# Sixteen basis sums of a weight pair moved to another phase, a room of its own for one pair, and two products swapped

## Chip, core and metric

One core of a Trainium2 chip runs the kernel. Time is device microseconds (us) from launch to end; lower is better. PE is TensorE, DVE is VectorE, ACT is ScalarE, POOL is GpSimd, and SP is the engine whose queue issues most DMAs.

## What is computed

A linear attention without softmax, normalized per head, then a SwiGLU feed-forward layer, all in 32-bit floats:

```
kv  = einsum('bhsd,bhse->bhde', k, v)           # 8 batches, 8 heads, 576 positions, 64 wide
out = einsum('bhsd,bhde->bhse', q, kv)
rms = sqrt(mean(out * out, axis=-1) + 1e-6)
x   = (out / rms * g_norm), heads side by side   # 4608 x 512
g, val = x @ w_gate, x @ w_val                   # 512 x 1536 each
result = (silu(g) * val) @ w_out                 # 1536 x 512
```

## The kernel before

The 4608 tokens go through in nine blocks of 512. Each block has an *up phase* (x times the gate and value weights, then silu and the product, which gives `h`, kept transposed as 12 slots of 128 rows) and a *down phase* (`h` times the output weights). Block 0 computes its up phase plainly. Blocks 1 and 2 use Strassen's method in Winograd's form: seven products in place of eight. Blocks 3 to 8 run in pairs and apply the method twice, one inside the other (class `Inner`, L807).

**Products and their order.** `Quad.multiply` (L661) issues one of the seven products P1 to P7. They are summed in PSUM in three banks: chain b takes P1, then P6, P7 and P4 on top; chain a takes P2; chain c takes P5, then P3 on top. Between two members of a chain the bank is read: after P7, ACT copies bank b (L711) and DVE adds bank c to the copy (`after7`), so P4 may write b only after the copy and P3 may write c only after the addition. `after4` (L724) takes silu on ACT and multiplies on POOL into the second half of the tokens of `h`; `after3` adds on DVE and multiplies on POOL into the first half. `h_sums` then forms two sums over `h` on DVE, which P5 and P6 of the down phase read.

In an up phase of blocks 1 and 2 there are six *weight pairs* (`j` = 0 to 5, called pair 1 to 6 in the change's name), each a unit `Up`. The order in `Up.sequence` is P1, P5, then P4 and P3 of the unit before, P6, P2, P7. After the last unit only its P4 and P3 are left. The down phase (`Ffn.down`) has a single unit: P1, P6, P5, P7, P2, P4, P3, 24 matmul records each; in between it calls steps of the next block's attention (`fill`): after P1 `whole` (heads, L431; squares, roots, scaling; transposes on DVE, L510), after P5 `place_x` (16 DMAs that put x in place, L522), after P2 `end` (gain on ACT, L529, and the sums over x on DVE).

**Basis sums.** The paired blocks need each weight pair as 7 x 7 pieces, sums of its quarters, in device memory (tensor `w`), from where a stream loads them. Blocks 1 and 2 make and send them on the side. For the products whose weights are themselves sums this is `leaf_steps`; for the others it is `kept_steps(j)`: two halves, each of four sums on DVE (three of 256 columns, one of 512) and two DMAs on SP, `(6,)` and `(7, 4, 5)` (L916). Its sums are written to a room, `xi_alone`, from which the DMAs read, so that the next pair's sum must wait until the DMA that reads the same piece has landed. Such steps stand in two lists, `making` and `later`; after each product `make` takes some of them (4 in block 1, 2 in block 2, 12 in a down phase), from `later` only when `making` is empty. Pairs 1 to 4 come in `later` of block 1, pairs 5 and 6 in `making` of block 2:

```
if p == 3:
    if self.j < NP - 2:
        ffn.later.extend(kept_steps(self.j))
...
for j in (NP - 2, NP - 1):
    ffn.making.extend(kept_steps(j))
```

**Rooms.** `ring()` gives one of five buffers of 128 x 2048 that rotate; the product units, the attention's q, squares and scaled heads, and `leaf_steps` all take them. `h_alone` holds `h` of blocks 0, 1 and 2; its last four slots belong to pairs 5 and 6 and are written late in an up phase.

**What sets the order.** Each engine's instructions are put in order by a scheduler from their place in the program and an estimate of when they can run; it may move an instruction ahead of others. `tc.issue_after(ins)` puts what is traced inside behind `ins` on `ins`'s engine. In block 2 DVE keeps program order through the up phase and PE through the whole block (`in_order`). A DMA waits on its queue for the landing of the eighth DMA before it, since there are eight landing semaphores in turn.

In block 2 the attention of block 3 is woven into the up phase by `ahead`: the visit of k and v (L370), 32 loads of q (L333, `load`), `turn_q` (transposes of q on DVE, L386), and `half`, the heads (L431) with what follows.

Of the kernel before, what the change touches and what calls it, by code (L numbers as in the profile page):

```python
# [14 lines left out]
P = 128  # L15
# [3 lines left out]
def kernel(  # L19
# [41 lines left out]
    nc = tc.nc  # L61
# [10 lines left out]
    NF = FF // P  # L72
    NP = NF // 2
# [35 lines left out]
    def span(at, size):  # L109

        return arena[:, int(at * KIB) : int((at + size) * KIB)]
# [8 lines left out]
    x_alone, xi_alone, h_alone = x_of(span(48, X)), xi_of(span(62, XI_)), h_of(span(73, H_))  # L120
# [31 lines left out]
    def ring():  # L152

        return r_pool.tile([P, 4, BLK], F32, name="r")
# [485 lines left out]
    class Quad:  # L640
# [11 lines left out]
        def multiply(self, p):  # L652
            name, first = CHAIN[p]
            if first:
                tiles = [PSUMS[name].tile([P, 2, HB], F32, name=name) for _ in range(1 + (name in self.apart))]
                self.ps[name], self.apart[name] = tiles[0], tiles[-1]
            banks = self.ps[name], self.apart[name]
            for e, i in self.order(p):
                lhsT, rhs = self.operands(p, e, i)

                self.ffn.multiplied = nc.tensor.matmul(  # L661
                    banks[e][:, e], lhsT=lhsT, rhs=rhs, start=first and i == 0 and (e == 0 or banks[0] is not banks[1]),
                    stop=i == self.steps - 1, skip_group_check=True,
                )
            getattr(self, f"after{p}", lambda: None)()
# [17 lines left out]
    class Up(Quad):  # L683
# [43 lines left out]
        def after3(self):  # L727
            add(nc.vector, self.u2, self.ps["c"], self.u2)
            mul(nc.gpsimd, self.h[:, :, 0:HB], self.s, self.u2)
            if self.j < NP - 1:  # L730
                self.ffn.owed = lambda: self.ffn.h_sums(self.j, 1, nc.vector)
            else:
                self.ffn.ended = self.ffn.h_sums(self.j, 1, nc.vector)

        def multiply(self, p):
            super().multiply(p)
            ffn = self.ffn
            if ffn.n == 1:
                if p == 5:
                    self.leaf_room = ring().rearrange("p f (s c) -> p (f s) c", c=P)  # L740
                if p in (5, 7, 4):
                    at = 3 * (5, 7, 4).index(p)
                    ffn.making.extend(leaf_steps(self.j, [(self.w[p].unsqueeze(1), (p,))], self.leaf_room[:, at:]))
                if p == 3:
                    if self.j < NP - 2:
                        ffn.later.extend(kept_steps(self.j))

    class Inner:

# [164 lines left out]
    def send_leaf(j, os, ps, src):  # L914
        dst = stream.dram[:, j, steps_of(OUTERS, os), steps_of(INNERS, ps)].rearrange("p o i c -> p o (i c)")
        tc.keep_in_program_order(nc.sync.dma_start(out=dst, in_=src))  # L916
# [20 lines left out]
    def kept(j):  # L937

        halves = lambda t: t[j].rearrange("p (o i) (e c) -> p o i e c", o=2, e=2)
        return [(halves(wg), (1, 2)), (halves(wv), (6, 3))]  # L940

    def raw_steps(j):


        for t, os in kept(j):
            yield lambda t=t, os=os: send_leaf(j, os, (1,), t[:, :, 0, 0])
            yield lambda t=t, os=os: send_leaf(j, os, (2, 3), t[:, :, 1].rearrange("p o e c -> p o (e c)"))

    def kept_steps(j):


        room = xi_alone.rearrange("p a b c -> p (a b) c")
        for i, (t, os) in enumerate(kept(j)):
            b11, b12, b22 = t[:, :, 0, 0], t[:, :, 0, 1], t[:, :, 1, 1]
            to = room[:, 8 * i : 8 * (i + 1)].rearrange("p (o r) c -> p o r c", r=4)
            t2_ = to[:, :, 0]
            yield lambda b22=b22, b12=b12, t2_=t2_: sub(nc.vector, t2_, b22, b12)
            yield lambda b11=b11, t2_=t2_: add(nc.vector, t2_, t2_, b11)
            yield lambda t=t, t2_=t2_, to=to: sub(
                nc.vector, to[:, :, 2:4], t[:, :, 1], t2_.unsqueeze(2).to_broadcast([P, 2, 2, P])  # L960
            )
            yield lambda t2_=t2_, os=os: send_leaf(j, os, (6,), t2_)
            yield lambda b11=b11, t2_=t2_, to=to: sub(nc.vector, to[:, :, 1], b11, t2_)
            yield lambda to=to, os=os: send_leaf(
                j, os, (7, 4, 5), to[:, :, 1:4].rearrange("p o r c -> p o (r c)")
            )
        if j < 2:
            yield from raw_steps(j)
# [90 lines left out]
    class Ffn:  # L1059
# [27 lines left out]
        def up(self, fill):  # L1087

            self.s1 = s_pool.tile([P, NP, HB], F32, name="s1")
            units = [Up(self, j) for j in range(NP)]  # L1090
            units[0].prepare()
            last = None
            for i, this in enumerate(units):
                if i + 1 < len(units):
                    units[i + 1].prepare()
                for unit, p in this.sequence(last):
                    if unit:
                        visited, self.visited = self.visited, None
                        with tc.issue_after(visited.ins) if visited else ExitStack():
                            unit.multiply(p)  # L1100
                        self.make(4 if self.n == 1 else 2)
                        for steps, most in ((self.chores, 2), (self.sends, 10)):
                            for _ in range(min(most, len(steps))):
                                steps.pop(0)()
                    fill.get((i, p) if unit is this else None, lambda: None)()
                last = this
            self.down_ = Down(self)
            self.down_.turn_t(5)
            for unit, p in last.sequence(None):
                if unit is None:  # L1110
                    last.multiply(p)

        def down(self, nxt, then={}):

            down = self.down_
            fill = nxt.steps() if nxt else {}
            for p in (1, 6, 5, 7, 2, 4, 3) if 5 in fill else (1, 5, 6, 7, 2, 4, 3):
                if p == 1 and 7 not in down.t:
                    down.turn_t(7, self.ended)
                if p == 6 and 4 not in down.t:  # L1120
                    down.turn_t(4, nxt.halves[0] if nxt and nxt.n >= TURNED else None)

                with tc.issue_after(nxt.multiplied.ins) if self.n == 0 and p in (5, 6) else ExitStack():
                    down.multiply(p)
                self.make(12)
                if p in fill:
                    fill[p]()
                if p in then:
                    then[p]()
                if p == 1:  # L1130

                    with tc.issue_after(nxt.q_turned.ins) if self.n == 0 else ExitStack():
                        down.turn_s3()
# [109 lines left out]
    def ahead(ffn, att, then):  # L1243

        def load(att, i):
            return lambda: ffn.sends.extend(att.quarter_steps(i, (0, 1), (nc.sync,)))

        def first():
            visit(ffn, att, (0, 1))
            ffn.sends += [load(att, 0), lambda: then.load_kv(0), load(att, 1)]  # L1250

        def turn(i):
            ffn.chores.append(lambda: att.turn_q(i))

        def second():
            visit(ffn, then, (0,), True)
            ffn.sends.append(lambda: then.load_kv(1))

        def half(i):
            with tc.issue_after(ffn.multiplied.ins):  # L1260
                att.heads(i, range(NS), (m_psum, m_psum))
            ffn.visited = att.multiplied
            ffn.chores += att.chores(i)
            if i:
                ffn.chores += att.turn_steps()

        def rest():
            for i in range(2):
                load(then, i)()

        def raw():
            for j in range(2, NP):
                ffn.sends += raw_steps(j)

        def sums():
            ffn.chores.extend(att.sum_steps())

        for j in (NP - 2, NP - 1):
            ffn.making.extend(kept_steps(j))

        return {
            (0, 1): first, (1, 6): lambda: turn(0), (1, 7): second, (2, 1): lambda: half(0), (2, 6): lambda: turn(1),
            (2, 7): rest, (3, 1): lambda: half(1), (3, 7): lambda: visit(ffn, then, (1,), True), (4, 1): att.place_x,
            (4, 2): raw, (4, 7): att.gain_x, (5, 5): sums,
        }
# [133 lines left out]
```

## Time and profile before

| | before |
|---|---|
| median of 7 runs | 1024.88 us |
| lowest, highest | 1021.78, 1026.1 us |
| the profiled execution, its span | 1025.69 us, 1023.9 us |
| PE busy | 999.3 us, 98% of the span |
| DVE busy | 660.5 us, 65% |
| POOL busy | 367.8 us, 36% |
| ACT busy | 232.6 us, 23% |
| DMA | 143.23 MB, 140 GB/s on average |

Line numbers (L661 and so on) are those printed above. An instruction's row names its start and duration in us, its engine (a `q` behind it is the engine's queue, which waits or issues a DMA; PEld is a weight load of PE), its line, the operation, what it writes and reads (`out<-in`, by the program's names without buffer numbers), its shape and how many were merged; in brackets stands the idle time of the engine before it and what ended that. A float product is two matmul records, 0.2158 us apart at full clock; 24 records of the down phase take 5.18 us, the 8 of an up product 1.73 us.

Where the two blocks lie: block 1's up phase from 156.2, its down phase from 228.1 (the first matmuls of P1 stand before P4 there) to 273.9; block 2's up phase to 361.3, its down phase to 399.8.

### The profile page before, as it was taken

How to read it: one execution, taken by the hardware profiler on the slowest of the kernel's cores; microseconds unless marked ns; L12 is line 12 of the kernel's file. 1: busy time of each engine (PE TensorE's matmuls, PEld its weight loads, DVE VectorE, ACT ScalarE, POOL GpSimd, SP SyncE). 2: the span in 40 equal slices, each digit the busy share in tenths (PEclk: the TensorE clock that was granted, in tenths of full speed). 3: DMA queues.
4: the chain of work that ended last, by engine and by line, in shares of the span. 5: the costliest groups of instructions: out<-in, count | busy, mean ns of one | idle time of the engine just before them, and what ended most of it. 6: DMA issues, size and time to landing. Idle time of an engine off the chain costs nothing.

```text
span 1023.9 us, 17080 instructions
## 1 busy us (share of the span) xinstructions
PE 999.3 (98%) x6506; PEld 833.4 (81%) x6506; DVE 660.5 (65%) x1118; ACT 232.6 (23%) x367; POOL 367.8 (36%) x290
## 2 busy tenths in 40 slices
PE   5999999998989999999999999999999999999998
PEld 4544688887878888888888888888888888888887
DVE  2999797779347475666666846666767566666211
ACT  2666112221122312121111212112112121121100
POOL 0000273534534240454556003554650026546600
PEclk9999999999999999999999999999999999999999
DMA  8689643666564845676753365667321654443011
GB/s 219 199 265 265 124 90 115 217 206 174 116 146 77 212 86 162 172 204 163 169 145 50 89 159 152 160 172 183 98 34 51 144 159 146 150 148 94 1 42 42
DMA packets 254290, 143.23 MB, mean 140 GB/s; under 512 B 149504, under 2 KB 236544, under 8 KB 254208
## 3 DMA queue, kind: packets, MB, share of 16 engines
q1 hardware_dynamic: 219264, 137.67, 49.8%
q10 hardware_dynamic: 34880, 4.46, 2.7%
q8 instruction: 52, 0.85, 0.3%
q14 instruction: 30, 0.25, 0.1%
q0 software_dynamic: 64, 0.00, 0.0%
HBM read 104.99 MB, written 28.70 MB: 131 GB/s over the span
## 4 chain that ended last, share of the span: by engine, by line
PE 79%; DVE 10%; DMA 3%; SPq 3%; ACT 1%; issue 1%; POOL 1%; DVEq 0%; POOLq 0%; ACTq 0%
PE b L661 22%; PE b L807 22%; PE c L661 12%; PE c L807 11%; PE a L661 6%; PE a L807 5%; SPq L333 2%; DVE r L190 2%; DVE arena L131 2%; PE m L431 1%; PE m L370 1%; DVE arena L199 1%; DVE r L184 1%; DMA arena<-in_v_dram 1%; DMA ld<-in_v_dram 1%
## 5 line engine op out<-in xcount | busy, mean ns | idle before, releaser
L807 PE MATMUL b<-arena,t 128*128 128x256 f32 x1008 | 244.5, 381 | 0.0
L807 PEld LDWEIGHTS b<-arena,t 128*128 128x128 f32 x1008 | 190.0, 190 | 29.6 <-DVE r L130 2.4
L130 POOL TENSOR_TENSOR r<-r 128x256 f32<-128x256 f32 (+1 forms) x90 | 94.9, 1056 | 246.6 <-DMA t<-w 149.5
L130 DVE TENSOR_TENSOR r<-c,r 128x512 f32<-128x512 f32 (+1 forms) x170 | 104.8, 625 | 114.1 <-PE c L807 41.1
L130 DVE TENSOR_TENSOR r<-b,r 128x512 f32<-128x512 f32 (+1 forms) x234 | 139.1, 607 | 59.9 <-PE b L807 54.7
L131 POOL TENSOR_TENSOR t<-wo 128x512 f32<-128x512 f32 x54 | 76.1, 1429 | 181.0 <-DVE wo L130 104.6
L132 POOL TENSOR_TENSOR arena<-r 128x1024 f32<-128x1024 f32 (+1 forms) x54 | 101.7, 1897 | 104.3 <-DVE r L130 72.3
L130 DVE TENSOR_TENSOR r<-a,r 128x512 f32<-128x512 f32 x93 | 59.2, 637 | 114.3 <-PE a L661 77.6
L131 DVE TENSOR_TENSOR arena<-arena 128x512 f32<-128x512 f32 (+3 forms) x102 | 106.8, 1057 | 27.8 <-PE b L661 13.7
L807 PE MATMUL c<-arena,t 128*128 128x256 f32 x504 | 122.5, 379 | 0.8 <-ACT r L821 0.8
L807 PEld LDWEIGHTS c<-arena,t 128*128 128x128 f32 x504 | 95.6, 190 | 14.5 <-ACT r L821 1.2
L661 PE MATMUL b<-wo,arena 128*128 128x256 f32 x432 | 98.6, 382 | 2.6 <-issue 1.6
L661 PE MATMUL b<-t,arena 128*128 128x256 f32 x432 | 96.4, 379 | 1.4 <-POOL s L130 0.7
L661 PEld LDWEIGHTS b<-wo,arena 128*128 128x128 f32 x432 | 81.1, 190 | 15.3 <-issue 2.0
L661 PEld LDWEIGHTS b<-t,arena 128*128 128x128 f32 x432 | 81.9, 190 | 13.2 <-POOL s L130 1.1
L821 ACT COPY r<-b 128x512 f32<-128x512 f32 x54 | 31.7, 586 | 191.0 <-PE b L807 191.0
L131 POOL TENSOR_TENSOR t<-arena 128x512 f32<-128x512 f32 x36 | 50.4, 1412 | 63.5 <-PE c L661 26.0
L807 PE MATMUL a<-arena,t 128*128 128x256 f32 x252 | 66.1, 379 | 0.0
L807 PEld LDWEIGHTS a<-arena,t 128*128 128x128 f32 x252 | 47.9, 190 | 6.5
L661 PE MATMUL c<-wo,arena 128*128 128x256 f32 x216 | 48.2, 379 | 0.2 <-DVE r L130 0.2
L661 PE MATMUL c<-t,s 128*128 128x256 f32 x216 | 48.1, 379 | 0.0
L661 PE MATMUL a<-wo,arena 128*128 128x256 f32 x216 | 48.1, 379 | 0.0
(102 smaller groups left out, 1221.9 us busy)
## 6 DMA issues: line engine op xcount, KB each, us to landing
t<-w SPq DMA_DIRECT2D x180, 256.0 KB, 3.1
out_dram<-r SPq DMA_DIRECT2D x17, 512.0 KB, 2.9
ld<-in_k_dram SPq DMA_DIRECT2D x26, 288.0 KB, 4.8
ld<-in_v_dram SPq DMA_DIRECT2D x26, 288.0 KB, 5.9
t<-w SPq DMA_DIRECT2D x54, 128.0 KB, 2.2
ld<-in_moe_w_gate_dram SPq DMA_DIRECT2D x12, 512.0 KB, 4.9
ld<-in_moe_w_val_dram SPq DMA_DIRECT2D x12, 512.0 KB, 4.7
ld<-in_moe_w_out_dram SPq DMA_DIRECT2D x12, 512.0 KB, 5.0
```

The costliest lines, as they stand in the source:

```text
L130: add = lambda e, o, a, b: e.tensor_tensor(out=o, in0=a, in1=b, op=OP.add)
L131: sub = lambda e, o, a, b: e.tensor_tensor(out=o, in0=a, in1=b, op=OP.subtract)
L132: mul = lambda e, o, a, b: e.tensor_tensor(out=o, in0=a, in1=b, op=OP.mult)
L184: nc.vector.tensor_scalar(out=mag.bitcast(F32), in0=mag.bitcast(F32), scalar1=self.LOW, scalar2=self.HIGH, op0=OP.max, op1=OP.min,)
L190: return nc.vector.scalar_tensor_tensor(out=mag, in0=mag, scalar=3, in1=sign, op0=OP.logical_shift_left, op1=OP.bitwise_xor)
L199: return nc.vector.tensor_tensor(out=dst.bitcast(U32), in0=self.mag.rearrange("p (a b) -> p a b", a=a, b=b), in1=unit.bitcast(U32).rearran ...
L333: queue.dma_start(out=to[32 * r : 32 * (r + 1), j, g0:g1], in_=q[b, 4 * i + 2 * j + h, s0 : s0 + 32 * (g1 - g0), 32 * d : 32 * (d + 1)].re ...
L370: self.positions = nc.tensor.matmul(self.kv_ps[r][u * D : (u + 1) * D, g, :], lhsT=k[:, u, c, :], rhs=v[:, u, c, :], start=(c == 0), stop= ...
L431: self.multiplied = nc.tensor.matmul(self.ps[i][u][p : p + D, t, j, :], lhsT=self.qt[rows, tile_t, head, p : p + D], rhs=kvs[b % 3][rows, ...
L661: self.ffn.multiplied = nc.tensor.matmul(banks[e][:, e], lhsT=lhsT, rhs=rhs, start=first and i == 0 and (e == 0 or banks[0] is not banks[1 ...
L807: self.ffn.multiplied = nc.tensor.matmul(ps[:, i], lhsT=stream.use(self.ffn.n, self.j, o, p), rhs=self.operand(o, p), start=first and i == ...
L821: nc.scalar.copy(out=dst, in_=ps)
```

## The change

Three edits.

1. *Pairs 3 and 4.* `kept_steps` of `j` = 2 and 3 no longer enter `later` in block 1's up phase. They are traced in block 1's down phase, behind P5 (pair 3, room `xi_alone`) and behind P7 (pair 4, room `ring()`), each behind the scaling of block 2's heads on DVE (`nxt.scaled`) and the last x transfer on SP (`nxt.placed`).
2. *Pair 6.* `kept_steps` takes its room as an argument; for `j` = 5 that is the last four slots of `h_alone`. Pair 5 keeps `xi_alone`.
3. *Last unit.* In blocks 1 and 2 the last unit issues P3, then P4, then `h_sums` (`Up.end`), where before it issued P4, then P3 with `h_sums` in `after3`.

```
@@ class Up
             if self.j < NP - 1:
                 self.ffn.owed = lambda: self.ffn.h_sums(self.j, 1, nc.vector)
-            else:
-                self.ffn.ended = self.ffn.h_sums(self.j, 1, nc.vector)
+
+        def end(self):
+
+            for p in (3, 4):
+                self.multiply(p)
+            self.ffn.ended = self.ffn.h_sums(self.j, 1, nc.vector)
...
                 if p == 3:
-                    if self.j < NP - 2:
-                        ffn.later.extend(kept_steps(self.j))
+                    if self.j < 2:
+                        ffn.later.extend(kept_steps(self.j, chunks(xi_alone)))
@@
-    def kept_steps(j):
-
-
-        room = xi_alone.rearrange("p a b c -> p (a b) c")
+    def chunks(t):
+
+        return t.rearrange("p f (s c) -> p (f s) c", c=P) if len(t.shape) == 3 else t.rearrange("p a b c -> p (a b) c")
+
+    def kept_steps(j, room):
+
+
@@ class Ffn, up
             self.down_.turn_t(5)
-            for unit, p in last.sequence(None):
-                if unit is None:
-                    last.multiply(p)
+            last.end()
@@ class Ffn, down
+                if p in (5, 7) and self.n == 1:
+
+                    with tc.issue_after(nxt.scaled.ins), tc.issue_after(nxt.placed.ins):
+                        for step in kept_steps(2 + (p == 7), chunks(ring() if p == 7 else xi_alone)):
+                            step()
@@ ahead
         for j in (NP - 2, NP - 1):
-            ffn.making.extend(kept_steps(j))
+            ffn.making.extend(kept_steps(j, chunks(h_alone[:, NF - 4 :]) if j == NP - 1 else chunks(xi_alone)))
```

## The prediction

> **What bounds the kernel.** TensorE (PE) is busy 999.3 of 1023.9 us, so only its idle stretches, and any stretch at a lower clock, can be won. I first listed who PE waited for between 100 and 400 us (blocks 1 and 2 run from 156 to 400); columns: total, times, longest, in us.
>
> ```profile
> PE m L431 <- DVE r L386: 3.3, 1, 3.3
> PE b L661 <- issue: 1.6, 1, 1.6
> PE b L661 <- POOL arena L132: 1.0, 1, 1.0
> PE b L661 <- ACT r L711: 0.8, 1, 0.8
> PE c L661 <- DVE r L130: 0.5, 2, 0.3
> ```
>
> Five lines, 7.2 us, and one of them is half. Then the timeline around it (start, duration, idle time before and what ended it):
>
> ```profile
> 298.17 1.99 PE L661 MATMUL b<-arena 128*128 128x256 f32 x8
> 301.47 0.69 DVE L131 TENSOR_TENSOR arena<-arena 128x512 f32<-128x512 f32 x1 [5.36 <-DMA w<-arena]
> 302.08 1.24 DVE L386 STREAM_TRANSPOSE r<-ld 128x1024 f32<-128x1024 f32 x1
> 303.46 1.98 PE L431 MATMUL m<-kv,r 64*64 64x64 f32 x64 [3.29 <-DVE r L386]
> 305.38 3.78 PE L661 MATMUL c<-arena,t 128*128 128x256 f32 x8
> ```
>
> The heads of block 3 (L431) wait for a transpose of q (L386). VectorE (DVE), whose order is fixed in block 2, stood 5.36 us in front of it, at a basis sum of pair 6 that wants to overwrite a piece of the shared room which a DMA of pair 5 has not yet sent. Next the sums by stretch (length, then busy us of PE, its weight loads, DVE, ACT, POOL; then granted clock, DMA share, GB/s):
>
> ```profile
> 300.20:303.40 3.20, 0.00 (x0) 0.00 (x0) 1.93 (x3) 0.59 (x1) 0.00 (x0) 0.89 0.95 287
> 303.40:309.50 6.10, 6.04 (x74) 5.14 (x75) 3.73 (x11) 1.09 (x2) 0.20 (x1) 0.50 0.73 204
> 309.50:315.00 5.50, 5.50 (x27) 4.85 (x26) 2.05 (x4) 0.99 (x2) 4.79 (x4) 1.00 0.85 128
> ```
>
> The wait is paid twice: after it the clock is 0.50 until 309.5, though PE is busy. The queue of SP shows why the DMA was late:
>
> ```profile
> 281.05 10.99 SPq L333 DMA_DIRECT2D ld<-in_q_dram  x20
> 292.15 0.40 SPq L916 DMA_DIRECT2D w<-arena  x1
> 298.81 0.41 SPq L916 DMA_DIRECT2D w<-arena  x1
> ```
>
> The sends stand between 32 loads of q. Last, where the moved sums go, the down phase of block 1, first DVE, then GpSimd (POOL):
>
> ```profile
> 251.69 2.36 DVE L510 STREAM_TRANSPOSE r<-r 128x1024 f32<-128x1024 f32 x2
> 253.97 2.34 DVE L131 TENSOR_TENSOR arena<-arena 128x512 f32<-128x512 f32 x2
> 263.54 0.69 DVE L130 TENSOR_TENSOR r<-a,r 128x512 f32<-128x512 f32 x1 [7.22 <-PE a L661]
> 264.14 1.75 DVE L131 TENSOR_TENSOR arena<-arena 128x1536 f32<-128x1536 f32 x1
> 265.81 0.69 DVE L130 TENSOR_TENSOR r<-c,r 128x512 f32<-128x512 f32 x1
> ```
> ```profile
> 251.85 4.18 POOL L131 TENSOR_TENSOR t<-wo 128x512 f32<-128x512 f32 x3 [9.12 <-DVE r L132]
> 256.00 7.58 POOL L131 TENSOR_TENSOR t<-arena 128x512 f32<-128x512 f32 x6
> 265.37 5.00 POOL L131 TENSOR_TENSOR t<-arena 128x512 f32<-128x512 f32 x3 [1.80 <-PE b L661]
> ```
>
> DVE has a hole of 7.22 us there, but POOL works through nearly all of it.
>
> **Part 1: a room of its own for pair 6.** The four sums of each half of pair 6 now write the end of h, free since block 1's P3 (ended 273.9). No sum before the transpose overwrites pair 5's unsent pieces, so the 5.36 us go. What is late next? The transpose needs the first 16 of the 32 q loads; SP had issued 20 by 292.04 and such a load lands in about 2 us, so the data is there by 294. On DVE it follows an addition that starts at 295.42 and takes 0.69, then one sum of 0.61: start 296.7, end 297.9. PE wants it at 300.16. Nothing is left of the wait, with 2 us to spare. Price: from the start of that unit's P1 to the start of P3 the chain of waits has 298.17 to 311.12, 12.95 us; the next unit, with the same heads in it, has 317.86 to 324.49, 6.63. **Gain 6.3**, of which 3.3 is the wait and 3.0 the slow clock and restart. Bounds: 6.3, or 0.3 if q's loads hold the transpose anyway (the last of 32 landed at 301.8).
>
> **Part 2: 16 sums and 8 DMAs leave block 1's up phase.** At its end DVE runs without a hole from 225.8 to 256.3. The addition of the last P3 starts at 235.41, though P3 was through by 233.2; POOL's product follows at 236.17, and PE's last four P1 matmuls at 237.60, 0.95 late. From 228.05 to 238.66 PE issues 40 matmuls, 8.63 us at 0.2158, so 1.98 us are lost. Sums of pairs 3 and 4 are what stands in front (0.4 to 0.7 each at 228.67, 229.11, 229.66, 233.54, 235.07).
>
> **Part 3: P3 ahead of P4.** P3 adds to bank c, which DVE must first read (the addition of after7), and that needs ACT's copy. P4 needs only the copy. Block 2 has PE in program order: P4 starts at 357.75 behind the copy, the addition starts at 357.63 and by block 1's row (230.46, PE at 231.20) releases PE 0.74 later, 358.37. **Loss 0.6.** In block 1 four P1 matmuls cover the wait until 228.92; copy (228.84) and addition end about 229.65, so some 0.9 with the restart is lost in place of 1.98. Behind P3 the addition and POOL's 1.37 end about 233.6, while P4 and P1 keep PE until 236. With parts 2 and 3 **block 1 gains 0.8** (bounds: a loss of 0.4 if the addition still starts at 230.46, a gain of 2.0 if nothing is lost).
>
> **Part 4: the sums in the down phase.** 16 instructions, 12 of 256 and 4 of 512 columns. By the quiet rows at 283.94 to 288.08 four take 1.87 us from start to start, so 7.5 in all, which the hole and the 2.3 us of pair 5's sums in front of it (they can't come before pair 3's any more) would hide. But a 256-column sum at 254.83 took 1.49 against 0.42, with POOL busy: each POOL instruction met adds about 1.07. Of the nine from 251.85 some seven remain at 253.97: 7.5 more, 15.0 in all.
>
> The Trainium skill speaks against this part too: "GPSIMD Engine Reference", section "Key points", has POOL share its SBUF interfaces with DVE instructions of two SBUF inputs. It gives no price. By the quiet rows alone part 4 would cost nothing and the whole sum would be 6.5, 1018.4; the page is on the side of the 1.49.
>
> DVE starts 3.2 us sooner, since three of pair 4's and 5's sums (238.35 to 241.52) no longer stand before the statistics of block 2's heads: 250.8, end 265.8. Then come the three instructions of 263.54 to 266.50, 3.0 us, with one or two of POOL's later ones: 269 to 270.5. P3 of the down phase needs the second and third of them; it started at 268.52, now 267.7. Wait 1.3 to 2.8 if all 16 stand in front, none if half do. I take a **loss of 1.2**. Bounds: 2.8 and then 2.9 for the slow clock, 5.7; or a gain of 1.8, if the 1.56 us without a releaser at 244.19 (a fetch behind the 288 KB loads, I suppose) goes with the shorter SP queue and nothing waits. If both happen the wait eats the gain. The eight sends (0.45 each, 3.6 us) lie on SP between the last x transfer (261.4) and the store it waits for (269.38); they read a ring buffer and the old room, and nobody asks for either before 283.
>
> On what a wait costs, the row says: 3.29 us idle brought the clock of 0.50, 1.56 us did not. The Trainium skill, "TensorE: Matmul & The Clock Gate", section "What's actually happening", puts the drop after an idle window of about 3.4 us that runs free. By that rule part 1 would be worth 3.3 to 6.3, as the window falls, and the sum 2.3 to 5.3; by the row it is 6.3, and the sum uses the row.
>
> **Sum.** 6.3 + 0.8 - 0.6 - 1.2 = 5.3 us. The profiled execution took 1025.69 (span 1023.9), so 1020.4; it lies 0.8 above the median of the runs, 1024.88, so **1019.6** is forecast. Own range 1016 to 1022.5.
>
> **Rivals.**
> A. *The wait stays, under another name.* For it: the chain of waits itself runs through a q load (299.76, 1.96 us) into the transpose. Against: that is one of the last two of 32, and the transpose starts 0.61 behind the sum, the ordinary step of two instructions. Gain 0.3 + 0.8 - 0.6 - 1.2: 1025.6; with no wait in the down phase 1024.4.
> B. *DVE becomes the bound in block 1's down phase* and the kernel is slower. Place: the three instructions before the down phase's P3, which have 2.0 us of slack now (266.50 to 268.52). Price: each us beyond it, and from some 3 us on 2.9 for the clock. It outweighs 6.5 when the wait passes 3.6 us, the sums ending 2.3 us later than I have them, as when POOL's three at 265.37 all fall in and the fetch wait is gone. A wait of 5.6 gives 6.5 - 8.5: 1026.9. For it: POOL's cover over the hole. Against: the earlier start, and that four sums behind the three instructions would end it.
> C. *The sums aren't where they are written.* The queues' order is made by a scheduler, as pair 5's first sums show, which lie in block 1's down phase though block 2 traces them. Sums or sends put in front of the q loads would give back about half: 1022.
>
> **Numbers.** Forecast 0.65, A 0.14, B 0.14, C 0.07. Faster by over 0.2% (2 us, about what a measurement of this kernel can tell from no change) takes the forecast and C, 0.72; within 0.2% A, 0.14; slower B, 0.14. The range goes from 1015.5 (the gains 6.3, 2.0 and 1.8 less 0.6) to 1025: it leaves out B and part of A.
>
> **What would show it.** No wait of L431 on L386 near 297 and the clock at 1.00 through 310: part 1. PE waiting for the c addition before P3 at both ends of the up phases, about 1.3 us in block 2: part 3. DVE full from 251 to 267 and PE's wait before the last 24 matmuls of the down phase: part 4. I am wrong if a half-clock stretch is still there, wherever it is.

## The result and the profile after

| | before | after |
|---|---|---|
| median | 1024.35 us (36 runs) | 1027.12 us (15 runs) |
| lowest, highest | 1021.44, 1026.72 us | 1026.04, 1029.59 us |
| the profiled execution, its span | 1025.69, 1023.9 us | 1029.51, 1027.7 us |
| PE busy, DVE busy | 999.3, 660.5 us | 998.9, 668.1 us |

The change makes the kernel slower: the ratio of after to before is 1.0033 with a 95% interval from 1.0025 to 1.0041, some 2.8 us by the medians. The forecast was 1019.6. (The 7 runs of before in the table above are the first of these 36.)

The waits of PE between 100 and 400 us (total, times, longest) show what went and what came. The heads' wait of 3.3 us is gone (the 1.6 that are left are two waits at 124 and 125 us, ahead of the blocks that change), and a wait of 8.2 us before a product into bank c is new:

```profile
PE c L661 <- DVE r L130: 8.9, 3, 8.2
PE m L431 <- DVE r L386: 1.6, 2, 1.3
PE b L661 <- issue: 0.5, 1, 0.5
```

Where the old wait stood, the timeline of after (start, duration, idle before and its releaser) runs on without one. The transposition of q starts at 296.69, and P5 follows the heads at 301.25, where it stood at 305.38 before:

```profile
296.69 1.24 DVE L386 STREAM_TRANSPOSE r<-ld 128x1024 f32<-128x1024 f32 x1
...
298.24 1.99 PE L661 MATMUL b<-arena 128*128 128x256 f32 x8
300.16 1.16 PE L431 MATMUL m<-kv,r 64*64 64x64 f32 x64
301.25 1.99 PE L661 MATMUL c<-arena,t 128*128 128x256 f32 x8
...
304.81 1.89 PE L661 MATMUL c<-arena 128*128 128x256 f32 x8
```

The new wait stands 50 us later, between the last unit's P7 and its P3. The timeline of after there, three engines together:

```profile
347.42 0.59 ACT L681 COPY r<-b 128x512 f32<-128x512 f32 x1 [2.86 <-PE b L661]
...
348.94 1.89 PE L661 MATMUL b<-arena,t 128*128 128x256 f32 x8
350.87 0.59 ACT L711 COPY r<-b 128x512 f32<-128x512 f32 x1 [2.87 <-PE b L661]
351.35 2.19 ACT L529 ACTIVATE arena<-arena,gain 128x1024 f32<-128x1024 f32 x2
353.57 0.69 DVE L130 TENSOR_TENSOR arena<-arena 128x512 f32<-128x512 f32 x1 [10.37 <-DMA w<-arena]
...
358.26 0.68 DVE L130 TENSOR_TENSOR r<-c,r 128x512 f32<-128x512 f32 x1
358.99 3.78 PE L661 MATMUL c<-arena 128*128 128x256 f32 x8 [8.15 <-DVE r L130]
...
365.40 4.91 PE L661 MATMUL b<-wo,arena 128*128 128x256 f32 x22
```

And the same rows of before, where P7 ran 6.15 us later:

```profile
346.73 0.59 ACT L677 COPY r<-b 128x512 f32<-128x512 f32 x1 [0.69 <-PE b L661]
347.21 2.19 ACT L529 ACTIVATE arena<-arena,gain 128x1024 f32<-128x1024 f32 x2
349.44 0.69 DVE L130 TENSOR_TENSOR arena<-arena 128x512 f32<-128x512 f32 x1
...
353.56 0.59 ACT L681 COPY r<-b 128x512 f32<-128x512 f32 x1 [2.86 <-PE b L661]
355.09 1.89 PE L661 MATMUL b<-arena,t 128*128 128x256 f32 x8
...
357.02 0.59 ACT L711 COPY r<-b 128x512 f32<-128x512 f32 x1 [2.87 <-PE b L661]
357.63 0.69 DVE L130 TENSOR_TENSOR r<-c,r 128x512 f32<-128x512 f32 x1 [1.65 <-ACT r L711]
...
361.27 5.34 PE L661 MATMUL b<-wo,arena 128*128 128x256 f32 x24
```

The later DVE row in each fence, 358.26 and 357.63, is the addition of after7, which P3 waits for. DVE keeps program order in block 2, and ahead of that addition it has the first sums over block 3's x (the row at 353.57, at 349.44 before). Before, ACT multiplied x by the gain (L529) right behind its copy of the last unit's P1 (L677), so ahead of its copies of P6 (L681) and P7 (L711). After, the same two instructions stand behind the copy of P7, although ACT stood idle for 2.86 and 2.87 us ahead of the copies at 347.42 and 350.87, and x had been in place since about 344 (the last of its 16 transfers was issued at 341.9; they took 2.0 to 2.6 us to land). So DVE stands 10.37 us at the sum. From the start of P7 to the start of the down phase's P1 it takes 16.46 us (348.94 to 365.40) where before it took 6.18 (355.09 to 361.27): 10.28 us lost.

The order of the transfers had changed too. SP, which sends half of x, stands 8.5 us among the q loads that go ahead of it, until the first x transfer of ACT's queue has landed (issued at 327.30; SP goes on at 329.62). Before has no such wait. So the last transfer of x is issued at 341.9, at 340.7 before, although PE is 6 us ahead: x itself came no sooner.

The clock takes its share, as the stretches of after show, where the old half-clock stretch was and at the new wait (length, busy us of PE, its weight loads, DVE, ACT, POOL, then granted clock, DMA share, GB/s):

```profile
303.50:306.00 2.50, 2.50 (x13) 2.20 (x12) 2.36 (x5) 0.60 (x1) 2.11 (x2) 1.00 0.82 240
...
351.00:354.50 3.50, 0.00 (x0) 0.00 (x0) 0.93 (x2) 2.54 (x3) 0.00 (x0) 1.00 0.97 282
354.75:364.75 10.00, 5.76 (x14) 4.60 (x15) 5.60 (x9) 0.63 (x1) 2.76 (x2) 0.50 0.97 215
365.00:367.00 2.00, 2.00 (x11) 1.77 (x10) 0.00 (x0) 0.60 (x1) 0.73 (x1) 1.00 0.00 0
```

The half-clock stretch of before is gone, and a longer one has come. The books of the two profiled executions close: 2.1 us later at the first matmul of block 1's down phase (230.15 against 228.05; this differs from run to run, since e1 and e10 below, whose edits lie behind this place, have 228.44 and 227.63), 2.0 won between there and block 2, 6.4 won at the heads, 10.3 lost here: 4.0 us more, against 3.8 measured (1029.51 less 1025.69).

### The profile page after: what moved, and what is told of

Its sections match the earlier page's. It is cut to its first block, busy times and chain, and to the rows that moved or that the text cites. A ratio compares the mean times of both kernels' runs of the same rounds, so it can differ in the third digit from the quotient of the medians.

```text
span 1027.7 us, 17091 instructions
## 1 busy us (share of the span) xinstructions
PE 998.9 (97%) x6506; PEld 833.4 (81%) x6506; DVE 668.1 (65%) x1118; ACT 232.7 (23%) x367; POOL 370.7 (36%) x290
## 4 chain that ended last, share of the span: by engine, by line
PE 86%; DVE 5%; SPq 3%; DMA 2%; POOL 1%; ACT 1%; issue 1%; DVEq 0%; POOLq 0%; ACTq 0%
PE b L811 21%; PE b L661 21%; PE c L661 12%; PE c L811 11%; PE a L661 5%; PE a L811 5%; PE b L1154 4%; PE c L1154 4%; PE m L431 1%; DVE arena L131 1%; SPq L333 1%; PE m L370 1%; DMA arena<-in_v_dram 1%; POOL t L131 1%; SPq L920 1%
## 5 line engine op out<-in xcount | busy, mean ns | idle before, releaser
L131 POOL TENSOR_TENSOR t<-wo 128x512 f32<-128x512 f32 x54 | 78.2, 1468 | 176.4 <-DVE wo L130 107.6
```

The lines of the kernel that those rows point to most:

```text
L131: sub = lambda e, o, a, b: e.tensor_tensor(out=o, in0=a, in1=b, op=OP.subtract)
```

## The experiments

Two questions had to be settled. *Why does DVE stand for 10.37 us?* My theory is the gain on ACT. The rival is what the profile names: the landing of a DMA `w<-arena`, one of the raw weight sends that fill the queues then. And *which edit does it?* Each kernel was timed beside runs of the kernel before on the same chip; their medians were 1024.96 us beside e1 to e4, 1024.44 beside e5 to e8 and 1025.15 beside e9 to e12, so ratios are compared rather than medians.

| run | edits (1 sums, 2 room, 3 swap) | gain on ACT | median, us | ratio to before, 95% |
|---|---|---|---|---|
| after | 1, 2, 3 | behind P7's copy | 1027.12 | 1.0033 (1.0025–1.0041) |
| e1 | 1, 2, 3 | held early | 1018.68 | 0.9934 (0.9915–0.9953) |
| e2 | 1, 2 | behind P7's copy | 1025.64 | 1.0004 (0.9990–1.0019) |
| e3 | 2 | behind P7's copy | 1026.86 | 1.0016 (1.0004–1.0028) |
| e4 | none | held late | 1033.67 | 1.0072 (1.0049–1.0096) |
| e5 | 2 | held early | 1019.44 | 0.9953 (0.9937–0.9969) |
| e6 | 1, 2 | held early | 1018.06 | 0.9938 (0.9922–0.9955) |
| e7 | 3 | early by itself | 1023.40 | 0.9994 (0.9979–1.0008) |
| e8 | 1 | early by itself | 1025.61 | 1.0013 (1.0004–1.0023) |
| e9 | 1, 2, 3 in block 1 alone | held early | 1017.20 | 0.9925 (0.9909–0.9941) |
| e10 | 1, 2, 3 | later still, x sums later too | 1018.03 | 0.9934 (0.9917–0.9950) |
| e11 | 1, 3 | early by itself | 1026.17 | 1.0014 (1.0002–1.0027) |
| e12 | 2, 3 | held early | 1017.66 | 0.9936 (0.9918–0.9955) |

### The gain alone, both ways (e1, e4)

e1 is after with one order added: the last unit's P6, and with it ACT's copy of P6, is traced behind the gain.

```
-                nc.scalar.activation(out=x, in_=x, func=ACT.Copy, scale=gain)
+                self.gained = nc.scalar.activation(out=x, in_=x, func=ACT.Copy, scale=gain)
@@ class Ffn, up
+                        gained = getattr(blocks[PAIRED], "gained", None) if (i, p) == (NP - 1, 6) else None
+                        with tc.issue_after(gained.ins) if gained else ExitStack():
...
                             unit.multiply(p)
```

> The changed kernel, with one order added: ACT takes the two gain instructions over block 3's x ahead of its copy of P6 of the last unit in block 2. Theory (the gain's late place on ACT holds VectorE at the first sum over x, with the addition behind it that P3 waits for): the wait of P3 falls from 8.15 us to about 1.3, no half-clock stretch is left, and from the start of that unit's P7 to the start of the down phase's P1 it takes some 6.5 us in place of 16.5: about 1017 us, 7 below the kernel before. Rival (VectorE waited for the landing of the raw weight sends, as the profile labels it): the wait and the half clock stay, about 1027 us.

The timeline of e1 at the same place:

```profile
343.01 2.19 ACT L529 ACTIVATE arena<-arena,gain 128x1024 f32<-128x1024 f32 x2
345.23 0.69 DVE L130 TENSOR_TENSOR arena<-arena 128x512 f32<-128x512 f32 x1 [3.63 <-ACT arena L529]
...
347.33 1.89 PE L661 MATMUL b<-arena,t 128*128 128x256 f32 x8
...
349.92 0.68 DVE L130 TENSOR_TENSOR r<-c,r 128x512 f32<-128x512 f32 x1
350.65 1.99 PE L661 MATMUL c<-arena 128*128 128x256 f32 x8 [1.42 <-DVE r L130]
...
354.20 5.34 PE L661 MATMUL b<-wo,arena 128*128 128x256 f32 x24
```

The sums start as soon as the gain is through, P3 waits 1.42 us, P7 to P1 takes 6.87 us, and the profiled execution has a granted clock of 1.00 throughout. The median is 1018.68, 6.3 us below its own runs of before, where after was 2.8 above its own: some 9 us apart, and the rows have 9.59 (16.46 less 6.87). The 16 raw sends are all still there (issued from 341.08 to 350.60, in after from 342.56 to 352.10), so they were not what DVE waited for, and nothing in the data holds the gain back to P7.

e4 is the converse: the kernel before, none of the edits in it, with the gain put behind P7's copy.

```
-                nc.scalar.activation(out=x, in_=x, func=ACT.Copy, scale=gain)
+                self.gains = getattr(self, "gains", []) + [nc.scalar.activation(out=x, in_=x, func=ACT.Copy, scale=gain)]
@@ class Up, after7
             copied = nc.scalar.copy(out=self.u3, in_=self.ps["b"])
+            for late in blocks[PAIRED].gains if self.ffn.n == 2 and self.j == NP - 1 else []:
+                tc.add_manual_dep(
+                    late.ins, copied.ins.name,
+                    mybir.DependencyInfo(mybir.DependencyClass.NoSync, mybir.DependencyReason.DATA), reason="order",
+                )
```

> The kernel before, none of the three edits, with one order added: ACT takes the two gain instructions over block 3's x behind its copy of P7 of the last unit in block 2. Theory: P3 of the last unit waits some 6 us for the addition behind the sums over x, with a half-clock stretch after it, besides the old one at the heads: some 8.6 us slower, about 1033 us. Rival (the raw sends' landing sets that wait): nothing changes by over 1 us, 1024 to 1025 us.

```profile
357.90 0.59 ACT L711 COPY r<-b 128x512 f32<-128x512 f32 x1 [2.87 <-PE b L661]
358.39 2.19 ACT L529 ACTIVATE arena<-arena,gain 128x1024 f32<-128x1024 f32 x2
360.61 0.69 DVE L130 TENSOR_TENSOR arena<-arena 128x512 f32<-128x512 f32 x1 [10.36 <-ACT arena L529]
...
366.02 3.78 PE L661 MATMUL c<-arena 128*128 128x256 f32 x8 [5.42 <-DVE r L130]
```

1033.67 us, 8.7 above before by the medians (5.0 to 9.8 by the interval) where 8.6 was worked out. The wait of DVE is the same to 0.01 us, and here the profile names L529. The DMA that it names in after is no evidence against this: in after, e2, e3, e9 and e10, labelled with a DMA, as in e1 and e4, labelled with L529, the first x sum starts 0.03 to 0.04 us after the gain has ended. The cause of the loss is settled: two instructions of ACT, 2.19 us together, at another place in its order.

### Which edit moves the gain, and what the swap adds (e3, e2, e7, e8, e11)

e3 is before with edit 2 alone, and e2 is after without edit 3:

```
-            ffn.making.extend(kept_steps(j))
+            ffn.making.extend(kept_steps(j, chunks(h_alone[:, NF - 4 :]) if j == NP - 1 else chunks(xi_alone)))
```
```
-            last.end()
+            for unit, p in last.sequence(None):
+                if unit is None:
+                    last.multiply(p)
```

> The kernel before with edit 2 alone (the room of its own for pair 6). Theory: the heads' wait and the first half-clock stretch go (6.4 us gained), but the gain over x goes late in ACT's order, P3 of the last unit waits some 6 us and a new half-clock stretch follows (8.6 lost): about 1026.5 us. Rival (the late wait comes from the other two edits): about 1018 us.

> The changed kernel with the last unit's order put back to P4, P3 (edits 1 and 2 stay; the gain stays late). Theory: P4 runs at once after P7, but P3 waits for the same late addition, some 6 us, and a half-clock stretch follows it still; 2 us less than the changed kernel, about 1025 us. Rival (the swap is what made the wait): no wait over 1 us, no half clock, about 1018 us.

1026.86 and 1025.64: both within 0.7 us of the theory and far from the rival. In e2 P4 goes first, yet P3 still waits for the addition, and the clock halves all the same:

```profile
350.89 1.97 PE L661 MATMUL b<-arena,t 128*128 128x256 f32 x8 [0.77 <-ACT r L711]
...
358.28 3.78 PE L661 MATMUL c<-arena 128*128 128x256 f32 x8 [5.42 <-DVE r L130]
```

So the swap lengthens the wait (8.15 against 5.42) but does not make it. e7, e8 and e11 leave edit 2 out of after, by this line; e7 leaves out edit 1 as well, and e8 edit 3 (as in e2):

```
-            ffn.making.extend(kept_steps(j, chunks(h_alone[:, NF - 4 :]) if j == NP - 1 else chunks(xi_alone)))
+            ffn.making.extend(kept_steps(j, chunks(xi_alone)))
```

> The kernel before with edit 3 alone (P3 ahead of P4 in the last units of blocks 1 and 2). Theory: both half-clock stretches stand as before; block 2 loses 0.6 (P3 waits for the addition), block 1 gains up to 1 (POOL's product no longer ends last): 1024 to 1025 us, no difference that can be measured. Rival (the swap by itself makes the wait of 8 us): 1030 us or more.

> The kernel before with edit 1 alone (16 sums and 8 DMAs into block 1's down phase). Theory: the waits at the end of block 1's up phase shrink by up to 1 us, no wait of the down phase's P3 on VectorE, the heads' wait and its half clock stay: 1023.5 us. Rival (the prediction's part 4: 15 us of sums make VectorE late in the down phase): P3 of the down phase waits 1.2 us or more, 1025 to 1027 us.

> Edits 1 and 3 without edit 2 (pair 6 in the shared room as before). Theory: block 1 ends up to 2 us earlier, but the heads of block 2's up phase wait for the same DMA and their wait grows by as much (5 us), with its half clock; the gain stays early in ACT's order: 1024 to 1026 us. Rival (block 1's 2 us come through to the end): 1022.5 us.

1023.40, 1025.61 and 1026.17. e7 can't be told from before. e8 is 0.13% slower where I had expected 1023.5, a miss. Its time is in the rival's range, but not for the rival's reason, since P3 of the down phase waits for nothing. The time goes at the heads: P1 of the unit whose heads wait starts 1.65 us earlier than before (296.52 against 298.17), and the heads wait that much longer, since the sum that holds DVE is let go at 301.75, against 301.47 before.

```profile
296.52 1.99 PE L661 MATMUL b<-arena 128*128 128x256 f32 x8
...
301.75 0.69 DVE L131 TENSOR_TENSOR arena<-arena 128x512 f32<-128x512 f32 x1 [5.69 <-DMA w<-arena]
...
303.74 1.99 PE L431 MATMUL m<-kv,r 64*64 64x64 f32 x64 [5.22 <-DVE r L386]
```

What block 1 wins is lost again at a wait whose end a DMA dates; e11 shows the same with a wait of 4.99 us. In e7, e8, e11 and before the gain stands ahead of P6's copy; in e2, e3 and after, the three kernels with edit 2 and no order added, it stands behind P7's copy. So edit 2 is what moves it, though nothing in edit 2 touches ACT or x. The wait of SP for an x transfer goes with it: 8.5 to 12.0 us in all nine kernels with edit 2, none in the five without. Since the order of ACT is made from estimates of when an instruction can run, I take it that the estimate changed; this is not shown, and it was not tried further.

### By which way the late gain hurts (e10)

e10 leaves the gain late, and traces the sums over x behind the last unit's P7, so behind the addition in DVE's order:

```
-            (4, 2): raw, (4, 7): att.gain_x, (5, 5): sums,
+            (4, 2): raw, (4, 7): att.gain_x, (5, 7): att.sums,
```

> The changed kernel with the sums over block 3's x traced behind the last unit's P7 (so on VectorE behind the addition that P3 waits for), the gain left as late on ACT as the scheduler puts it. Theory (the late gain hurts only through the sums that stand ahead of the addition on VectorE): P3 of the last unit waits about 1.4 us, no half clock is left, 1018.5 us. Rival (the late gain delays the last unit on ACT itself): a wait of several us stays, 1024 us or more.

```profile
349.08 0.69 DVE L130 TENSOR_TENSOR r<-c,r 128x512 f32<-128x512 f32 x1 [1.58 <-ACT r L711]
...
351.68 0.69 DVE L130 TENSOR_TENSOR arena<-arena 128x512 f32<-128x512 f32 x1 [1.05 <-DMA w<-arena]
```
```profile
349.47 2.18 ACT L529 ACTIVATE arena<-arena,gain 128x1024 f32<-128x1024 f32 x2
```

The gain runs at 349.47, later than P7's copy, and it costs nothing: 1018.03 us, with P3 waiting 1.40. So the late gain hurts only where DVE has its reader in front of the addition.

### What the three edits are worth without it (e5, e6, e12, e9)

All have e1's order. e5 has edit 2 alone, e6 edits 1 and 2, e12 edits 2 and 3; e9 is e1 with the swap in block 1 only:

```
-            for p in (3, 4):
+            for p in (3, 4) if self.ffn.n == 1 else (4, 3):
                 self.multiply(p)
```

> The kernel before with edit 2 alone, and the gain over block 3's x held ahead of ACT's copy of P6 of the last unit in block 2. Theory: the 6.4 us of the heads' wait are all there is to win here, and none is given back: 1018 us, and no half-clock stretch. Rival (the gain of the experiment with all three edits and the early gain came from edits 1 and 3 as well): 1020 us or more.

> Edits 1 and 2 with the early gain, the last unit in the order P4, P3. Theory: in block 2 P4 waits 0.8 us for ACT's copy and P3 for nothing, 0.7 less than with the swap; the stretch of 0.5 to 1.9 us without a releaser in block 1's down phase is long without the swap: 1017.5 to 1019 us. Rival (the swap pays): 1019.5 or more.

> Edits 2 and 3 without edit 1, with the early gain. Theory: against all three edits with the early gain (1018.7) it lacks only what edit 1 takes from block 1's up phase, some 0.6 us at the wait of the last unit's P3: 1019 to 1019.5 us. Rival (edit 1 is worth the 2 us it leaves off VectorE): 1020.5 us.

> Edits 1 and 2, the swap in block 1 alone (block 2's last unit has P4, P3), and the gain over block 3's x held ahead of ACT's copy of P6 of the last unit. Theory (the swap in block 1 is what shortens the stretch without a releaser in its down phase, from 1.4 to 1.9 us to 0 to 0.6, and in block 2 it costs 0.7): about 1017 us, below both kernels and below every kernel so far, with that stretch at 0.6 or less. Rival (that stretch has nothing to do with the swap in block 1): it is 1.4 us or more, and the time 1018 to 1018.5 us.

1019.44, 1018.06, 1017.66 and 1017.20. e5's time lies between theory (1018) and rival (1020 or more), so it settles little by itself; e6 and e9 are as expected. Edit 2 gives most of it: 0.47% (0.31 to 0.63), 4.8 us. What the others add is within the intervals, so rows have to say it. From the first matmul of the down phase's P1 in block 1 to the first of its P5 it takes 19.75 us before (228.05 to 247.80), 18.05 with edit 1 alone (e8), 17.70 with edit 3 alone (e7) and 17.71 with both (after): each gives about 2 us there, and together no more than one. That fits e12, which lacks edit 1 and is no slower than e1; my 19 to 19.5 for it was too high. In block 2 the swap costs 0.7: P7 to P1 takes 6.87 in e1 and 6.18 in e6 and e9. e9 has the lowest median of all, 0.75% below before (0.59 to 0.91); by the intervals it can't be told from e1, e6, e10 and e12.

## Why the prediction was wrong

The forecast was 1019.6, a gain of 5.3 us; 1027.12 was measured, a loss of 2.8. Step by step:

- **Part 1, the heads: right.** The transposition starts at 296.69 (296.7 was forecast), and from P1 to P3 the unit takes 6.57 us (298.24 to 304.81) where it took 12.95: 6.4 won, 6.3 forecast.
- **Part 1, "What is late next?": the step that failed.** It was asked once, at the heads, and answered "Nothing is left of the wait, with 2 us to spare". The sum then carried the 6.3 to the end of the kernel, with each engine's order of before, and charged the end of block 2 with part 3's 0.6 alone. It held until P7 at 348.94. But P3 hangs on the addition, the addition in DVE's order on the x sums, and these on the gain, which edit 2 had put behind the copy of P7: from the gain's start (351.35) to the addition's (358.26) it takes 6.91 us. So the place lost 10.28 us, 9.7 more than part 3 had there. It was the order, and not a lack of room: with the gain early (e1) the addition starts 0.70 us after P7 ends, before 0.65, and the win comes through. But no room is left over: DVE's idle time between the first x sum and the addition was 3.25 us before (1.11, 0.49 and, at the last row, 1.65) and is nil in e1.
- **Part 3, block 2: right in kind, and its 0.6 is 0.7** once the gain is early (6.87 less 6.18). But it took the addition's start from before, 357.63, and moved it along with P7; that DVE's order could hold it was not looked at.
- **Parts 2 and 3, block 1: right.** 0.8 was forecast for the last products; from the first matmul of P1 to the first of P6 it takes 12.63 us before (228.05 to 240.68) and 11.67 after: 0.96. The 1.56 us without a releaser, which stood in part 4 as a bound, fell to 0.48: 1.1 more.
- **Part 4: the sums were sized well, the loss of 1.2 did not come.** DVE in after:

```profile
252.03 2.07 DVE L131 TENSOR_TENSOR arena<-arena 128x256 f32<-128x256 f32 x2
254.03 2.89 DVE L130 TENSOR_TENSOR arena<-arena 128x256 f32<-128x256 f32 x2
256.84 6.24 DVE L131 TENSOR_TENSOR arena<-arena 128x512 f32<-128x512 f32 x4
263.60 0.69 DVE L130 TENSOR_TENSOR r<-a,r 128x512 f32<-128x512 f32 x1 [0.52 <-PE a L661]
264.21 1.75 DVE L131 TENSOR_TENSOR arena<-arena 128x1536 f32<-128x1536 f32 x1
265.87 0.69 DVE L130 TENSOR_TENSOR r<-c,r 128x512 f32<-128x512 f32 x1
266.47 2.30 DVE L131 TENSOR_TENSOR r<-arena 128x256 f32<-128x256 f32 x2
```

Pair 3's eight sums take 11.05 us (252.03 to 263.08) in place of 3.74 quiet ones; the 7.3 more are what seven POOL instructions at 1.07 were to add (7.5). But pair 4's eight, which write the ring's room, were put behind the three instructions that P3 needs (266.47), the case "none if half do", and P3 waits for nothing. On POOL's part in it the rows side with the Trainium skill's "GPSIMD Engine Reference", section "Key points", which has POOL share its SBUF interfaces with such DVE instructions.
- **The rivals.** A and B were waits at the wrong places; that B's 1026.9 is near the measured time is chance, for the wait that it priced did not come. C had the right cause, an order made by a scheduler, but looked only at the moved sums and sends and priced it at half of part 1; what was moved was an instruction that the change doesn't name. The last sentence of the prediction held: a half-clock stretch was still there.

Put together: 1019.6, and 9.7 for block 2's end, less 1.2 that part 4 did not cost, less 1.1 for the shorter stretch without a releaser and 0.3 for the small terms, is 1026.7; 1027.12 was measured.

## What to carry to other kernels

When a wait is taken away, list every wait behind it whose end a DMA or another engine dates, and move the work up to each of them in turn: what PE wins is kept only as far as the first that has less to spare. Where a scheduler orders an engine, an edit can reorder instructions that it doesn't touch, so compare each engine's order of instructions around the waits before pricing; an instruction that something critical hangs on through another engine's program order deserves an order of its own (here one `issue_after` was worth some 9 us). And a releaser's name in a profile is a hint, not proof: the same wait of 10.4 us was labelled a DMA in one kernel and ACT in another. What settled it was moving the instruction, both ways.

## What the hardware showed that was not expected

**The half clock comes in lengths of some 3.4 us.** In e7 the heads wait 3.16 us, and the clock is down from 302.1 to 305.5:

```profile
302.00:302.25 0.25, 0.00 (x0) 0.00 (x0) 0.25 (x1) 0.00 (x0) 0.00 (x0) 0.76 0.95 303
302.25:305.50 3.25, 2.90 (x66) 2.66 (x67) 2.06 (x6) 0.83 (x2) 0.00 (x0) 0.50 0.58 165
305.50:305.75 0.25, 0.25 (x2) 0.21 (x1) 0.25 (x1) 0.25 (x1) 0.00 (x0) 0.92 1.10 381
```

By slices of 0.25 us that is 3.41 us at half clock. In before, after a wait of 3.29, it is 6.83 us (302.6 to 309.4); after waits of 5.0 to 5.4 us also 6.8 (e2, e3, e4, e8, e11); after the 8.15 of after 10.2. These are one, two and three times 3.41. The Trainium skill, "TensorE: Matmul & The Clock Gate", section "What's actually happening", has a window of 3413 ns that runs free, and the rows agree with it: two waits that differ by 0.13 us cost one window and two. So the price of 3.0 us that part 1 put on the clock and the restart is one draw, not a constant; waits of 1.4 to 1.9 us brought no half clock in any run. PE need not stand idle for a whole window before the drop: in the 3.50 us ahead of 302.50 in before it was busy for 1.17.

**A product stops in the middle, and the swap in block 1 shortens the stop.** The profile names no releaser for it. P6 of block 1's down phase halts after 15 of its 24 records. In the seven kernels with P4 ahead of P3 in block 1 (before, e2 to e6, e8) the halt is 1.4 to 1.9 us; in the seven with P3 first (after, e1, e7, e9 to e12) it is 0 to 0.8. In e9:

```profile
239.75 3.50 PE L661 MATMUL b<-wo,arena 128*128 128x256 f32 x15
...
243.85 2.21 PE L661 MATMUL b<-wo,arena 128*128 128x256 f32 x9 [0.59 <-issue]
```

The prediction supposed a fetch behind the 288 KB loads, which the shorter queue of SP would take away. e8 has that queue and a halt of 1.6, so the queue is not it. For a fetch the traces do speak. The DMA queue that they call `q8 instruction` makes 52 transfers of 16 KB in the whole of before, 65 bytes for each of PE's 13012 matmuls and weight loads, and one of them starts near this product in every kernel:

| kernels | the transfer starts, before the 16th record is due | halt |
|---|---|---|
| P4 first (before, e2 to e6, e8) | 0.3 to 0.8 us | 1.4 to 1.9 us |
| P3 first, with edit 1 (after, e1, e9 to e11) | 1.7 to 2.0 us | 0.5 to 0.8 us |
| P3 first, without edit 1 (e7, e12) | 2.6 and 3.2 us | no halt; P6 is 0.1 and 0.2 us longer |

In the twelve kernels that halt, PE goes on 2.3 to 2.9 us after the transfer's start. So the halt looks like PE waiting for its next instructions. No run moved that transfer alone, so this is not shown, and why the order of two earlier products makes it start sooner stays open.
